# Weight splits and block sums of a dense layer made in the key-value stage and kept in DRAM, with three more weight pairs through seven block products

## The chip, the cores and the metric

The kernel runs on one core of one Trainium2 chip. Five engines of the core appear below: PE (TensorE, the matrix unit, whose weight loads are listed apart as PEld), DVE (VectorE), ACT (ScalarE), POOL (GpSimd) and SP (SyncE, which here only issues DMAs). Arrays live in DRAM, in SBUF (128 partitions) or, for results of matmuls, in PSUM, which is made of banks of 512 fp32 numbers per partition. The metric is the time on the device of one execution, in microseconds.

## The reference

Two layers read the same input and are mixed by a gate.

```python
def A(x, wqkv, w_phi, wo):               # linear attention, H = 32 heads of 20
    q, k, v = split(x @ wqkv)            # x is 1 x 2048 x 640, wqkv 640 x 1920
    pq, pk = q @ w_phi, k @ w_phi        # per head, 20 x 20
    phi_q = concat(softmax(pq), softmax(-pq))   # 40 features a head
    phi_k = concat(softmax(pk), softmax(-pk))
    kv = einsum("bhsf,bhsd->bhfd", phi_k, v)    # summed over all 2048 tokens
    z  = einsum("bhsf->bhf", phi_k)
    o = (phi_q @ kv) / (phi_q @ z + 1e-6)
    return o @ wo                        # wo 640 x 640

def B(x, w1, w2):                        # dense layer: w1 640 x 1728, w2 1728 x 640
    return silu(x @ w1) @ w2

g = sigmoid((x * gate_w).sum(-1))
return g * A(x) + (1 - g) * B(x)
```

All in fp32. The kernel reaches that accuracy with matmuls in a faster type: every operand is *split* into a high part (a rounded copy, made on ScalarE) and a low part (the operand minus its high part, made on VectorE or POOL), and a product is three matmuls: high by high, high by low, low by high.

## The kernel before, in words

Tokens come in 16 tiles of 128 for the keys and values, and in 4 blocks of 512 for the dense layer, worked on in two halves of two blocks. The 1728 columns of `w1` (rows of `w2`) are 13 chunks of 128 and one of 64; chunks 0 to 9 form the five *pairs* p = 0..4, chunks 10 to 13 are done singly.

The stages, with their places in the trace:

- **Start**, 0 to 32 us: key and value weights are split, tiles 0 and 1 are projected.
- **Key-value stage**, 32 to about 168 us, one token tile after another. For tile t, PE projects the tile into three PSUM banks, named `kvp_75`, `kvp_76` and `kvp_77` in the orders below, of 480, 500 and 302 columns (`kv_proj`, L566, 45 matmuls); these hold the keys' features (columns 0 to 639), the values and the gate's sum. VectorE takes each head's largest and smallest feature and subtracts (`k_spikes`, L581 to L588, first for columns 0 to 479, then 480 to 639); ScalarE copies the values (`v_part`, L399) and takes the exponential (L728); VectorE sums and takes reciprocals (`k_sums`, L592, L593); POOL scales the whole tile `ek` by these (L594). Two tiles later PE adds the products of `ek` and the values to `kvt` (`kv_acc`, L553). A bank is written anew only when it has been read, so the first bank of tile t+1 waits for the first four `k_spikes` instructions of tile t. Between them, every second tile has the next tokens split (`load_x`, L192 on ScalarE, L194 on POOL), and the others one of nine weight chunks that are wanted early (`load_f`: the list `PRE`, of `w2`'s chunks 10 to 13 and of `w1`'s 0 and 10 to 13).
- **Head**, 168 to about 232 us, and then ten **periods** n = 1..10. In period n the first product of pair n (`x @ w1`, first half of the tokens for n = 0..4, second for n = 5..9) and the second product (`@ w2`) of the pair before it are made side by side.
- **Tail** (500 to 560 us) and the queries with the output projection (560 to 728 us).

The first product of a pair over a half, 2 x 2 blocks, is always made with seven block products in place of eight, Strassen's scheme in a variant: `pair_mm`, banks `a`, `b`, `c`, `d`, 54 matmuls of 128x512. It needs sums of the weights' blocks as well as the weights. `pair_weights` makes them in the first half: both row chunks are loaded, ScalarE and POOL split them, POOL forms four block sums (L862), and these are split too (L865, L866); the results are stored to DRAM (`w_d`), and `pair_weights_again` loads them in the second half.

The second product is made in one of two ways. `out_items` makes ten sums of six matmuls (60, L1053), each added to an accumulator by VectorE (L1058). `sevens` uses seven block products here too (42 matmuls, L1094, and 12 for the fifth column block, L1116: 54 in all), with evictions at L1084; it needs block sums of `w2` (`block_sums`, L918 on POOL, L923 on ScalarE, L924 on VectorE) and sums of the dense layer's middle values (`t_sum`, `t_hi`, `t_lo`). Before the change `NSEV = 4`: pairs 0 to 3 of the second half go by `sevens`, all others by `out_items`. `block_sums` runs in periods 1 to 3 of the first half, and its results too are kept in DRAM (`s_d`) for the second half.

From the head on, the order of the instructions of PE, ACT, DVE and POOL is the order in which the program is written, and that is a string of names per period: `O1` to `O10`, with `HEAD`, `PASS` (last token tile and start of the head) and `TAIL`. In them `P1m` is the matmuls of the first block product of `pair_mm` and `P1p` what follows on other engines; `6am` and `6ae` are matmuls and eviction of the sixth block product of `sevens`, column blocks a (`b`: the other two); `y0m`, `y1m` are the fifth column block's; `o3m`, `o3e` those of `out_items`; `w0` ... are steps of the weights of the next pair, `c0` ... loads of `w2`, `s0`, `s1` loads of block sums, `b0` ..., `d0` ... steps of `block_sums`, `t2`, `h2`, `l2` sums of the middle values and their high and low parts. In the key-value stage the order is kept on ACT, DVE and POOL, but not on PE, where the scheduler takes what is ready by its own estimate. SP's DMAs stand in one queue in the order in which the program comes to them.

Of the kernel before, what the change touches and what calls it, by code (L numbers as in the profile page):

```python
# [16 lines left out]
P = 128  # L17
S = 2048
D = 640
# [41 lines left out]
NEARLY = 3  # L61
TAIL = """
dm0 fl4 da0 wa fl1 fl2 fm0 fl3 dm1 fs0 fm1 fs1 fl5 da1 dm2 ol1 W fm2 da2 dm3 fm3 fs2 fs3 da3 ol3 dm4
fm4 hm012 fm5 fs4 hm013 km wb fs5 hp012 hm113 wc hm112 kp hp013 hp113 ol0 da4 qp12 q012 q112 os1 wd
hp112 qe12 im0 qn12 ol4 qs12 ia0 qN12 im1 qc12 qp13 ig0 q013 ia1 qP12 im2 qi12 q113 ia2 qw12 qe13
qs13 qm12 ol2 qc13 im3 qn13 ia3 ig1 qN13 qP13 qp14 os0 os2 ig2 qi13 q014 im4 q114 qw13 ig3 xl0 ia4
qm13 im5 os3 qe14 qs14 qn14 qc14 xl1 qp15 ia5 qN14 xs0 xs1 qP14 q015 ig4 qi14 im6 tm0 xl2 q115 tm1
to0 qw14 qm14 os4 qe15 to1 ia6 qs15 qc15 qn15 im7 ia7 ig5 tm2 im8 ig6 ia8 im9 qN15 xs2 qP15 tm3 ig7
qi15 qw15 ia9 to2 ig8 to3 ig9 qm15
"""  # L70
PASS = """
wh h0a h0b us0 h1a uh0 h1b wl ka us1 uh1 ul0 ul1 h2a h2b us2 h3a xh1 xh3 uh2 h3b xh4 xl3 kb xh0 xl0
ko0 xl1 us3 xh2 ko1 xl2 ko3 ko2 ul2 xl4
"""
HEAD = """
w0 gs P1m P1p rs r0 w1 w2 w3 P2m hm10 hm12 w4 P2p dm0 r1 ks0 w5 w6 w7 w8 s10 ks1 w9 s30 s11 hp12 da0
ks2 mg dm1 ks3 s20 w10 w11 da1 dm2 da2 s40 dm3 s31 s21 s41 da3 st p31 hm13 p10 p40 v0 p11 dm4 p20 p41
hp10 v1 hm11 hp11 hp13 v2 p21 v3 da4 P5m P5p P4m em0 p30 y0 v4 y1 y2 ea0 P4p em1 y3 P6m y4 ea1 y5 P6p
em2 P3m y6 y7 ea2 P3p y8 y9 P7m P7p em3 Cm ea3 y10 em4 y11 Cp ea4
"""  # L80
O1 = """
P1m P1p o0m b0 b1 o0e b2 b3 P2m P2p b4 b5 o1m o1e b6 b7 P5m P5p st b8 c0 o2m o2e c1 c2 c3 P4m P4p d0
o3m o3e d1 d2 P6m P6p d3 d4 o4m o4e d5 d6 P3m P3p d7 d8 o5m o5e P7m w0 w1 P7p w2 w3 o6m o6e w4 w5 o7m
o7e w6 w7 o8m o8e w8 w9 Cm Cp w10 w11 o9m o9e
"""
O2 = """
P1m o0m P1p c0 c1 o0e c2 c3 P2m P2p d0 d1 o1m o1e d2 d3 P5m P5p st d4 d5 o2m o2e d6 d7 P4m P4p w0 o3m
d8 o3e w1 P6m w2 P6p w3 w4 o4m o4e w5 w6 P3m P3p w7 w8 o5m o5e w9 w10 P7m P7p w11 o6m o6e o7m o7e o8m
o8e Cm Cp o9m o9e
"""  # L90
O3 = """
xl2 xl1 P1m P1p xl0 o0m c0 xu0 o0e o1m P2m o1e xu1 P2p c1 xu2 P5m st c2 P5p c3 o2m o2e d0 d1 P4m P4p
d2 d3 o3m d4 d5 o3e P6m P6p o4m d6 d7 o4e d8 w0 P3m P3p w1 w2 o5m o5e w3 w4 P7m P7p w5 w6 o6m o6e w7
w8 o7m o7e w9 o8m w10 o8e w11 Cm Cp o9m o9e
"""
O4 = """
r0 P1m P1p o0m g c0 o0e c1 P2m P2p r1 c2 o1m st s10 o1e c3 P5m o2m P5p o2e s11 P4m w0 P4p s30 w1 o3m
o3e s31 w2 P6m P6p s20 w3 o4m o4e s21 s40 P3m p10 P3p o5m s41 o5e p11 p40 P7m P7p p41 xl4 o6m o6e xu4
o7m o7e p21 p20 xl3 o8m o8e xu3 Cm Cp o9m o9e
"""  # L100
O5 = """
P1m P1p p30 p31 o0m o0e yl4 yu4 o1m o1e yl2 yu2 o2m o2e P2m P2p c0 yl3 yu3 c1 o3m w0 w1 P5m P5p st w2
w3 o3e o4m o4e P4m P4p P6m P6p o5m o5e P3m P3p o6m o6e P7m P7p o7m o7e o8m o8e Cm Cp o9m o9e
"""
# [30 lines left out]
def mix_kernel(ctx: ExitStack, tc: tile.TileContext, xT, wqT, wkc, wkr, wv, bd, bdc, cst, wo, w1, w1r, w2, out):  # L135
# [1697 lines left out]
```

## Time and profile before

| what | value |
|---|---|
| time, median of 3 runs | 730.0 us (729.78 to 730.61) |
| the profiled execution: its own time | 730.17 us |
| its span, first to last instruction | 728.4 us |
| granted TensorE clock, as a share of full speed | 1.00 |
| PE busy | 721.2 us, 99% of the span |
| DVE, POOL, ACT busy | 429.9, 395.6, 297.4 us |
| DMA | 98.80 MB, mean 136 GB/s |

Engines' rows give busy time, its share of the span and the number of instructions. In the tables by stage each row is a stretch of the span; after its length stand, for PE, PEld, DVE, ACT and POOL, busy time and number of instructions, then the granted clock, the busy share of the DMA engines and the GB/s moved. In the chain (the work that ended last, followed back) and in the timelines a row has its start, how long it took, and what it was, with `x6` for six instructions; what stands in brackets is how long the engine was idle before it and for whom it waited.

### The profile page before, as it was taken

To read this page: it belongs to the slowest core of one execution; us is meant where nothing else is said; L and a number is where in the kernel's file an instruction comes from. 1 tells how busy PE (TensorE), PEld (TensorE's weight loads), DVE (VectorE), ACT (ScalarE), POOL (GpSimd) and SP (SyncE) were. 2 spreads that over 40 slices of the span, in tenths; PEclk is the share of its full clock that TensorE was granted. 3 is DMA by queue.
4 is the path that set the end of the run, shared out by engine and by line. 5 is a ranking of instruction groups with operands and counts; after the bars stand their busy time and mean duration, and the time that the engine had idled before them with its cause. 6 is when DMAs were issued, how large, how long until landed. Compare 5 with 4: busy or idle time off the path is not lost.

```text
span 728.4 us, 12513 instructions
## 1 busy us (share of the span) xinstructions
PE 721.2 (99%) x4935; PEld 621.0 (85%) x4935; DVE 429.9 (59%) x708; ACT 297.4 (41%) x558; POOL 395.6 (54%) x307
## 2 busy tenths in 40 slices
PE   9999999999999999999999999999999999999998
PEld 8888888888888888888888788788997899999988
DVE  4565555565253557568525656653887766766652
ACT  5333322336466354435344323535334453435330
POOL 2354545534756475572766447311598867767440
PEclk9999999999999999999999999999999999999999
DMA  8111111114734577588965623342133332121222
GB/s 306 56 56 56 46 56 55 63 35 135 238 116 176 213 276 277 207 314 324 330 205 188 219 68 107 109 117 73 52 115 119 102 95 83 56 94 45 74 87 81
DMA packets 50751, 98.80 MB, mean 136 GB/s; under 512 B 6352, under 2 KB 25828, under 8 KB 50692
## 3 DMA queue, kind: packets, MB, share of 16 engines
q1 hardware_dynamic: 50692, 98.00, 40.0%
q8 instruction: 39, 0.64, 0.4%
q14 instruction: 20, 0.16, 0.1%
HBM read 66.15 MB, written 31.84 MB: 135 GB/s over the span
## 4 chain that ended last, share of the span: by engine, by line
PE 97%; DVE 1%; ACT 1%; DMA 1%; issue 0%; DVEq 0%; ACTq 0%
PE o L1053 18%; PE kvp L566 17%; PE pa L1629 10%; PE pq L542 9%; PE a L964 9%; PE o L1094 5%; PE ph L632 3%; PE c L964 3%; PE b L964 3%; PE d L964 3%; PE pn L1587 3%; PE pT L1480 2%; PE hp L651 2%; PE kvt L553 2%; PE o_m L1116 1%; PE kvp L440 1%
## 5 line engine op out<-in xcount | busy, mean ns | idle before, releaser
L1053 PE MATMUL o<-u,w 128*128 128x512 f32 x580 | 142.5, 391 | 0.0
L1053 PEld LDWEIGHTS o<-u,w 128*128 128x128 f32 x580 | 108.0, 188 | 22.7 <-DVE acc L1058 0.6
L566 PE MATMUL kvp<-wh,xa 128*128 128x480 f32 (+2 forms) x420 | 92.5, 360 | 0.0
L566 PEld LDWEIGHTS kvp<-wh,xa 128*128 128x128 f32 x420 | 72.8, 188 | 10.4
L1629 PE MATMUL pa<-oT,wo 128*128 128x256 f32 x600 | 77.1, 281 | 0.1
L363 POOL TENSOR_TENSOR w<-wr,w 128x640 fp32r<-128x640 f32 x26 | 41.8, 1615 | 64.5 <-ACT w L352 64.5
L1629 PEld LDWEIGHTS pa<-oT,wo 128*128 128x128 f32 x600 | 73.8, 188 | 1.1 <-DVE oT L1608 0.8
L1209 POOL TENSOR_TENSOR ez<-eq,zbc 128x1280 f32<-128x1280 f32 x16 | 48.0, 3002 | 47.6 <-DVE sm L1239 24.6
L594 POOL TENSOR_TENSOR ek<-ek,st 128x1280 f32<-128x1280 f32 x16 | 38.2, 2386 | 50.3 <-DVE st L593 42.1
L542 PE MATMUL pq<-wq,xb 128*128 128x320 f32 x360 | 55.9, 312 | 0.0
L542 PEld LDWEIGHTS pq<-wq,xb 128*128 128x128 f32 x360 | 52.9, 188 | 2.2 <-DVE oT L1608 2.0
L1058 DVE TENSOR_TENSOR acc<-acc,o 128x512 f32<-128x512 f32 x70 | 46.4, 679 | 14.2 <-PE o L1053 14.1
L978 ACT ACTIVATE v<-v 128x512 f32<-128x512 f32 x33 | 20.9, 632 | 82.9 <-DVE v L997 36.2
L194 POOL TENSOR_TENSOR xa<-xra,xa 128x512 fp32r<-128x512 f32 (+1 forms) x26 | 26.4, 1038 | 41.4 <-ACT xa L192 37.0
L566 PE MATMUL kvp<-wl,xa 128*128 128x480 f32 (+2 forms) x210 | 47.6, 356 | 0.0
L1192 ACT ACTIVATE eq<-eq 128x1280 f32<-128x1280 f32 x16 | 20.4, 1276 | 63.9 <-DVE eq L533 63.9
L980 DVE TENSOR_TENSOR u<-v,u 128x512 fp32r<-128x512 f32 x29 | 21.5, 742 | 34.4 <-ACT u L979 31.5
L399 ACT COPY v<-kvp 128x340 f32<-128x340 f32 (+1 forms) x30 | 12.5, 417 | 70.1 <-PE kvp L566 68.2
L566 PEld LDWEIGHTS kvp<-wl,xa 128*128 128x128 f32 x210 | 36.6, 188 | 4.8
L1084 DVE TENSOR_TENSOR acc<-acc,o 128x512 f32<-128x512 f32 x48 | 31.3, 682 | 15.6 <-PE o L1094 12.1
L1245 POOL TENSOR_TENSOR eq<-eq,sm 128x1280 f32<-128x1280 f32 x16 | 37.9, 2368 | 1.0 <-DVE sm L1239 0.8
L592 DVE TENSOR_REDUCE st<-ek 128x64 f32<-128x1280 f32 x16 | 23.8, 1487 | 22.7 <-ACT ek L728 21.3
(236 smaller groups left out, 1483.7 us busy)
## 6 DMA issues: line engine op xcount, KB each, us to landing
wr<-w SPq DMA_DIRECT2D x33, 320.0 KB
w_d<-w SPq DMA_DIRECT2D x15, 640.0 KB
xr<-xT SPq DMA_DIRECT2D x27, 256.0 KB
w<-w_d SPq DMA_DIRECT2D x10, 640.0 KB
fb_d<-acc SPq DMA_DIRECT2D x20, 256.0 KB
s_d<-s SPq DMA_DIRECT2D x8, 512.0 KB
sa<-s_d SPq DMA_DIRECT2D x8, 512.0 KB
y<-fb_d SPq DMA_DIRECT2D x16, 256.0 KB
```

What stands on the lines that cost most here:

```text
L363: eng.tensor_tensor(t[:, 1, :], r[:, :D], t[:, 0, :].bitcast(F32), op=ALU.subtract)
L542: nc.tensor.matmul(dst, xt[c][:, hx, :], w[:, c, hw, lo : lo + n], start=first, stop=(hx == 1 and c == NC - 1))
L566: nc.tensor.matmul(kv_cols(t, lo, hi), xt[c][:, hx, :], WKV[hw][:, c, w_cols(lo, hi)], start=(n == 0), stop=(n == 3 * NC - 1), skip_group_ ...
L594: nc.gpsimd.tensor_tensor(groups(e), groups(e), spread(st[:, 1, :]), op=ALU.mult)
L964: last["mm"] = nc.tensor.matmul(out, lhs, rhs, start=(first and i == 0), stop=(stop and i == len(todo) - 1), skip_group_check=True)
L1053: nc.tensor.matmul(o, lhs, rhs, start=(n == 0), stop=(n == len(todo) - 1))
L1058: nc.vector.tensor_tensor(acc[j][m], acc[j][m], o, op=ALU.add)
L1084: nc.vector.tensor_tensor(acc[j][m], acc[j][m], o, op=ALU.add)
L1094: nc.tensor.matmul(o, ws[hw], x()[hx], start=(first and i == 0), stop=(i == len(PASSES) - 1), skip_group_check=True)
L1209: nc.gpsimd.tensor_tensor(ez, Q[t]["e"], zbc, op=ALU.mult)
L1245: nc.gpsimd.tensor_tensor(groups(q["e"]), groups(q["e"]), spread(q["sm"][:, 2 * H : 4 * H]), op=ALU.mult)
L1629: nc.tensor.matmul(pa[:, a, :], wo_tile[0][:, c, hw, ds] if c < NG else WOR[:, ds], o[:, ho, c, :] if c < NG else o[:GW, ho, c, :], start= ...
```

## The change

Nothing is computed otherwise than before except that three more second products go by `sevens`; the rest is a move of work from the first half to the key-value stage.

- `NSEV = (3, 4)`: pairs 0 to 2 of the first half and 0 to 3 of the second go by `sevens`. PE's rows fall from 4267 to 4249 matmuls, those of `out_items` from 580 to 400, those of `sevens` rise from 168 to 294 and from 48 to 84.
- A new generator `weights_ahead` runs in the key-value stage. For pairs 1 to 4 it loads two chunks of `w1`, splits the first whole (`F`, 128x640) and the second's last 384 columns (`B`), makes four block sums on POOL (`R10` is sum 0 of pair 1) and splits these (`G`, 128x256 each); for pairs 0 to 4 it loads two chunks of `w2` and splits them (`U`), and for pairs 0 to 3 makes and splits the four block sums (`S`, `Y`). The high parts are copies on ScalarE, the low parts subtractions on VectorE. All go to DRAM. There are 14 splits of 128x640, 4 of 128x384, 32 of 128x256, and 32 block sums of 128x256; VectorE's instructions rise from 710 to 755 over the kernel, ACT's from 559 to 563, POOL's go from 310 to 298, SP's from 299 to 340.
- The order of the key-value stage is now a string `KV`: `T4` is the projection of tile 4 and the `kv_acc` of tile 2, `a4` and `b4` the two parts of `k_spikes`, `v4` the values, `e4` the exponential, `r4` sums and reciprocals, `m4` POOL's scaling, which is now placed apart from `r4`, `x4` and `l5` are `load_x` and `load_f`.
- The nine early chunks are stored to DRAM as well (`w_keep`) and loaded again where they were split a second time (`w_again`). In the first half `pair_weights_again`, `w2_again` and `sums_again` load what was made; `pair_weights` remains for n = 0 and n = 10, and the stores and `block_sums` of the first half are gone.
- All strings of orders are written anew.

Three places in the instructions' order follow. The first is VectorE in the key-value stage, from tile 4's maxima to tile 5's first (`mmk` holds the maxima and minima, `ek` the features, `st` the sums). Before:

```order
L581 TENSOR_REDUCE mmk_690<-kvp_75 128x24
L582 TENSOR_REDUCE mmk_690<-kvp_75 128x24
L587 TENSOR_TENSOR ek_691<-kvp_75,mmk_690 128x24x20
L588 TENSOR_TENSOR ek_691<-mmk_690,kvp_75 128x24x20
L581 TENSOR_REDUCE mmk_690<-kvp_76 128x8
L582 TENSOR_REDUCE mmk_690<-kvp_76 128x8
L587 TENSOR_TENSOR ek_691<-kvp_76,mmk_690 128x8x20
L588 TENSOR_TENSOR ek_691<-mmk_690,kvp_76 128x8x20
L592 TENSOR_REDUCE st_718<-ek_691 128x64
L593 RECIPROCAL st_718<-st_718 128x64
L581 TENSOR_REDUCE mmk_800<-kvp_75 128x24
```

After, from the last subtraction of tile 4 (`ra` are raw weight rows, `aw`, `awb`, `awc`, `awd` the tiles of split weights):

```order
L612 TENSOR_TENSOR ek_772<-mmk_771,kvp_76 128x8x20
L769 TENSOR_TENSOR aw_783<-ra_2_667,aw_783 128x640
L769 TENSOR_TENSOR awb_785<-ra_3_669,awb_785 128x384
L769 TENSOR_TENSOR awb_785<-ra_3_669,awb_785 128x256
L769 TENSOR_TENSOR awc_800<-ra_2_667,awc_800 128x256
L769 TENSOR_TENSOR awc_800<-ra_3_669,awc_800 128x256
L769 TENSOR_TENSOR awd_806<-ra_2_667,awd_806 128x256
L616 TENSOR_REDUCE st_827<-ek_772 128x64
L617 RECIPROCAL st_827<-st_827 128x64
L605 TENSOR_REDUCE mmk_909<-kvp_75 128x24
```

Six subtractions of weights now stand between tile 4's features and its sums, and ahead of tile 5's maxima.

The second place is PE at the start of tile 6 in the key-value stage (`wh`, `wl` are the parts of the key and value weights, `xa` the tokens). Before:

```order
L553 MATMUL kvt<-ek_482,v_103 21x40 x32
L566 MATMUL kvp_75<-wh,xa_0_704 128x480 x2
L566 MATMUL kvp_75<-wh,xa_2_709 128x480 x2
L566 MATMUL kvp_75<-wh,xa_4_714 128x480
L566 MATMUL kvp_75<-wl,xa_0_704 128x480 x2
```

After:

```order
L577 MATMUL kvt<-ek_534,v_112 21x40 x32
L590 MATMUL kvp_77<-wh,xa_0_813 128x302 x2
L590 MATMUL kvp_77<-wh,xa_2_818 128x302 x2
L590 MATMUL kvp_77<-wh,xa_4_823 128x302
L590 MATMUL kvp_77<-wl,xa_0_813 128x302 x2
L590 MATMUL kvp_77<-wl,xa_2_818 128x302 x2
L590 MATMUL kvp_77<-wl,xa_4_823 128x302
L590 MATMUL kvp_77<-wh,xa_0_813 128x302 x2
L590 MATMUL kvp_77<-wh,xa_2_818 128x302 x2
L590 MATMUL kvp_77<-wh,xa_4_823 128x302
L590 MATMUL kvp_75<-wh,xa_0_813 128x480 x2
```

The third bank is now filled first in tile 6, as it is in tile 13 and, for 10 of its 15 matmuls, in tile 3.

The third place is PE in period 7, a period of the second half that goes by `sevens` before and after (`o1_10` and `o1_11` are the banks of block product 1 for the column blocks a and b, to which products 6 and 5 are added; `ts0` and `ts1` are middle sums, `sa1_0` block sums of `w2`). Before:

```order
L1116 MATMUL o1_m1_3946<-u6_3_1_3850,w2_3_3735 128x512 x3
L1094 MATMUL o1_10_3881<-ts0_3597,sa1_0_3862 128x512 x3
L964 MATMUL a7_3854<-xo0_1871,wc7_3675 128x512 x6
L1094 MATMUL o1_11_3874<-ts0_3597,sa1_0_3862 128x512 x3
L1094 MATMUL o1_10_3881<-ts1_3598,sa1_0_3862 128x512 x3
L1094 MATMUL o1_11_3874<-ts1_3598,sa1_0_3862 128x512 x3
```

After:

```order
L1070 MATMUL d7_4055<-xf_2_4_3552,wb7_3793 128x512 x3
L1200 MATMUL o1_10_3995<-ts0_3711,sa1_0_3976 128x512 x3
L1200 MATMUL o1_11_3979<-ts0_3711,sa1_0_3976 128x512 x3
L1070 MATMUL a7_3968<-xo0_2162,wc7_3794 128x512 x6
L1200 MATMUL o1_10_3995<-ts1_3712,sa1_0_3976 128x512 x3
L1200 MATMUL o1_11_3979<-ts1_3712,sa1_0_3976 128x512 x3
```

The six matmuls of `pair_mm`'s sixth block product have moved between the two products that write `o1_10` and `o1_11`. On VectorE the eviction between these two products (`acc0_1`, second row) stood behind both evictions of the fifth column block (`acc0_4`, `acc1_4`); before:

```order
L1084 TENSOR_TENSOR acc0_4_2067<-acc0_4_2067,o1_m0_3926 128x512
L1084 TENSOR_TENSOR acc1_4_2071<-acc1_4_2071,o1_m1_3946 128x512
L1084 TENSOR_TENSOR acc0_1_2064<-acc0_1_2064,o1_10_3881 128x512
L1084 TENSOR_TENSOR acc0_3_2066<-acc0_3_2066,o1_11_3874 128x512
L1084 TENSOR_TENSOR acc1_1_2073<-acc1_1_2073,o1_10_3881 128x512
```

After it stands between them:

```order
L1103 TENSOR_TENSOR v1_7_3992<-v1_7_3992,b7_4006 128x512
L1190 TENSOR_TENSOR acc0_4_2359<-acc0_4_2359,o1_m0_4040 128x512
L1190 TENSOR_TENSOR acc0_1_2356<-acc0_1_2356,o1_10_3995 128x512
L1190 TENSOR_TENSOR acc1_4_2363<-acc1_4_2363,o1_m1_4047 128x512
L1190 TENSOR_TENSOR acc0_3_2358<-acc0_3_2358,o1_11_3979 128x512
```

It has moved ahead of one eviction. The diff, cut to its core:

```diff
-NSEV = 4
+NSEV = (3, 4)
+KV = """
...
+S02 S03 a3 b3 Y03h v3 R1 Y00h e3 Y00l Y02h Y03l Y02l Y01h Y01l m2 r3 m3 l3 T4 a4 b4 v4 F1h B1h e4 F1l
+B1l R10 R11 R12 Q1 R13 G13h G10h G13l G12h G10l G11h G12l G11l x4 r4 m4 T5 a5 b5 v5 U10h U11h e5 U11l
...
 O7 = """
-P1m t3 s0 w0 2am t2 1bm P1p 2ae 1am 1be 1ae 2bm h3 P2m st h2 s1 w1 P2p t4 l2 c0 2be P5m c1 P5p y0m
...
+P1m t3 s0 t2 1bm w0 2am P1p 2ae 1am 1be 1ae 2bm h3 P2m h2 w1 P2p c0 s1 t4 l2 2be P5m c1 P5p y0m y1m
...
+    def w_again(w, f, pool=None):
+        t = W[w, f] = w_tile(w, f, pool)
+        with tc.issue_after(last["x"].ins):
+            nc.sync.dma_start(w_flat(w, f, t), w_k[w, f] if (w, f) in w_k else w2_d[f].rearrange("p s d -> p (s d)"))
...
-        nc.gpsimd.tensor_tensor(groups(e), groups(e), spread(st[:, 1, :]), op=ALU.mult)
+        return lambda: nc.gpsimd.tensor_tensor(groups(e), groups(e), spread(st[:, 1, :]), op=ALU.mult)
...
+    def weights_ahead(ops):
+
+        def row(w, f):
+            r = ta.tile([P, D], F32, tag="wr", name=f"ra{w}_{f}", bufs=4)
+            nc.sync.dma_start(r, w1[f] if w == 1 else w2[f * P : (f + 1) * P, :])
+            return r
+
+        def out(name, n):
+            return ta.tile([P, 2 * D], F32R, tag="wk", name=name, bufs=3)[:, :n]
...
+            def hi():
+                d[:] = dst()
+                nc.scalar.copy(d[0], src())
+
+            def lo():
+                eng.tensor_tensor(d[1], src(), d[0].bitcast(F32), op=ALU.subtract)
+                if done:
+                    keep(*done())
...
+                        nc.gpsimd.tensor_tensor(q[i], q[a], q[b], op=op)
...
     with inorder(ACT, DVE, POOL):
-        for t in range(NT - 1):
+        ops, scaled = {}, {}
...
+        weights_ahead(ops)
+        for name in KV.split():
...
+            ops.pop(name)()
...
     def pair_weights(n):
...
-        p = n if n < NPAIR - 1 else n - (NPAIR - 1)
+        p = n and NPAIR - 1
...
-        sev = NPAIR - 1 <= n < NPAIR - 1 + NSEV
+        sev = n < 2 * NPAIR - 2 and p < NSEV[h]
...
-            if NPAIR - 1 < n < NPAIR + NSEV:
+            if n < 2 * NPAIR - 2 and n != NPAIR - 1 and q < NSEV[n > NPAIR - 1]:
                 sevens(q, n == NPAIR)
...
-            if NPAIR - 2 < n < 2 * NPAIR - 2:
-                named("c0 c1", w2_again(2 * p, 2 * p + 1))
-            else:
-                named("c0 c1 c2 c3", w2_loads(2 * p, 2 * p + 1))
-            if NPAIR - 3 < n < 2 * NPAIR - 3:
+            named("c0 c1", w2_again(2 * p, 2 * p + 1))
+            if n < 2 * NPAIR - 3:
                 named("w0 w1 w2 w3", pair_weights_again(n + 1))
...
-            if n == 1:
-                named(" ".join(f"b{k}" for k in range(9)), block_sums(0))
-            if n < NSEV:
-                named(" ".join(f"d{k}" for k in range(9)), block_sums(n))
```

341 lines of the change are left out of this document (195 added, 146 removed).

## Prediction

> **What bounds the kernel now.** I read the engines' totals first, then PE's waits, then the table by stage, then the chain and single tiles. The totals of the page:
>
> ```profile
> span 728.4 us, 12513 instructions
> ...
> PE 721.2 (99%) x4935; PEld 621.0 (85%) x4935; DVE 429.9 (59%) x708; ACT 297.4 (41%) x558; POOL 395.6 (54%) x307
> ```
>
> PE is busy for all but 7.2 us. Its listed waits, first and last of five, the longest 1.1 us:
>
> ```profile
> PE warm L410 <- DVE ones L234: 1.1, 1, 1.1
> ...
> PE a L964 <- DVE v L1027: 0.2, 1, 0.2
> ```
>
> No large stall is there to remove, so only fewer matmuls or shorter gaps between them can save time, and a new wait anywhere adds in full. The table by stage has the key-value stage, the last two periods of the first half and the first two of the second:
>
> ```profile
> 61.00:168.00 107.00, 107.00 (x1222) 92.75 (x1209) 63.73 (x114) 35.10 (x71) 50.95 (x33) 1.00 0.20 58
> ...
> 314.00:340.00 26.00, 26.00 (x115) 21.13 (x114) 18.79 (x28) 11.54 (x22) 10.58 (x8) 1.00 0.91 330
> 340.00:366.00 26.00, 26.00 (x117) 21.50 (x116) 16.58 (x25) 8.29 (x15) 19.32 (x14) 1.00 0.92 335
> ...
> 391.00:416.00 25.00, 24.90 (x109) 19.87 (x108) 14.92 (x24) 8.34 (x14) 12.95 (x11) 1.00 0.52 170
> ```
>
> In the key-value stage PE is never idle, the others are busy 60% (DVE), 33% (ACT) and 48% (POOL), and DMA moves 58 GB/s. The granted clock is 1.00 in all rows, so no term below comes from it.
>
> **Fewer matmuls.** The chain has the price of one and the length of the periods (start, duration, what):
>
> ```profile
> 245.22 1.36 PE o L1053 x6
> ...
> 283.52 1.36 PE a L964 x6
> ...
> 309.36 1.36 PE a L964 x6
> ...
> 361.37 1.36 PE a L964 x6
> ...
> 385.51 2.04 PE a L964 x9
> ...
> 410.59 2.04 PE a L964 x9
> ...
> 435.80 2.04 PE a L964 x9
> ...
> 462.11 1.36 PE a L964 x6
> ```
>
> Six matmuls in 1.36 us are 0.2267 us each. From 283.52 to 309.36 a period by `out_items` takes 25.84, which is its 54 + 60 = 114 matmuls at that price: PE has no gap there. By `sevens` it has 108. Three pairs more are 18 matmuls fewer, **-4.08 us**, all of it on the path, since PE sets the end.
>
> But the four periods that go by `sevens` now are not gapless. Rows with x9 hold three matmuls of the last product ahead of the new pair's six, so those pairs begin 0.68 later, at 386.19, 411.27 and 436.48. The periods last 24.82, 25.08, 25.21 and 25.63; 108 matmuls are 24.48. Lost are 0.34, 0.60, 0.73 and 1.15, together 2.82. One of the places, from the chain in period 7:
>
> ```profile
> 400.67 0.69 PE o L1094 x3
> 401.37 0.02 issue
> 401.39 0.70 DVE acc L1084
> 402.09 0.04 issue
> 402.13 0.96 PE o L1094 x3
> ```
>
> PE waits 0.76 for VectorE to empty a bank to which the next product is added. I take for each of the three new periods the smallest loss seen, 0.34, as their orders are of the same kind as the new ones of the second half: **+1.02 us**; the bounds are 0 and 1.15 each (0 to 3.45). They have less to do besides than the periods of before: block sums and splits are gone from them.
>
> **The new orders of the second half.** In period 7 six matmuls of `pair_mm` (1.36 us) now stand between the two products, and the bank's eviction has moved ahead of another of 0.70. It can begin when its product ends and is done after 0.70 plus what is left of the one before: at most 1.4 us, against 1.36 of cover. The wait of 0.76 should go nearly whole. I take all four periods at 0.34, a gain of 0.26 + 0.39 + 0.81 = **-1.46 us**; bounds are no gap at all (-2.82) and new gaps of the same size as the old elsewhere (+0.5, about one stall of the kind).
>
> **The work in the key-value stage.** Before, one tile there (80.47 to 90.11) looks like this: projection from the chain, then rows of single engines (what stands in brackets is idle time and its cause):
>
> ```profile
> 80.47 8.93 PE kvp L566 x45
> 90.11 8.93 PE kvp L566 x45
> ```
>
> ```profile
> 81.59 3.24 POOL L194 TENSOR_TENSOR xa<-xra,xa 128x512 fp32r<-128x512 f32 x3 [4.45 <-ACT xa L192]
> 84.78 2.37 POOL L594 TENSOR_TENSOR ek<-ek,st 128x1280 f32<-128x1280 f32 x1
> ```
>
> ```profile
> 83.96 0.66 DVE L581 TENSOR_REDUCE mmk<-kvp 128x24 f32<-128x480 f32 x1 [1.16 <-PE kvp L566]
> ...
> 85.67 0.64 DVE L588 TENSOR_TENSOR ek<-mmk,kvp 128x480 f32<-128x480 f32 x1
> 87.90 0.33 DVE L581 TENSOR_REDUCE mmk<-kvp 128x8 f32<-128x160 f32 x1 [1.59 <-ACT v L399]
> ...
> 90.32 1.49 DVE L592 TENSOR_REDUCE st<-ek 128x64 f32<-128x1280 f32 x1 [1.41 <-ACT ek L728]
> 91.84 0.55 DVE L593 RECIPROCAL st<-st 128x64 f32<-128x64 f32 x1
> ```
>
> A tile lasts 9.65 us. By the stage's row VectorE works 63.73/107 of it, 5.75 us; ScalarE 3.17; POOL 4.60. Prices for what is added, from the same instructions elsewhere (duration in ns: least, median, most):
>
> ```profile
> L924 DVE TENSOR_TENSOR s<-wr,s x16: 410/420/1781, 235.0 to 300.8; 128x256 fp32r<-128x256 f32 x16
> ```
>
> ```profile
> L194 DVE TENSOR_TENSOR wo<-wo,wo x5: 815/875/2568, 514.3 to 546.0; 128x640 fp32r<-128x640 f32 x5
> L194 DVE TENSOR_TENSOR xf<-xrf,xf x4: 628/676/2850, 159.9 to 163.8; 128x512 fp32r<-128x512 f32 x4
> ```
>
> ```profile
> L352 ACT CAST w<-wr x28: 712/732/743, 35.9 to 508.5; 128x640 fp32r<-128x640 f32 x28
> ```
>
> ```profile
> L923 ACT CAST s<-wr x16: 400/402/407, 234.1 to 299.9; 128x256 fp32r<-128x256 f32 x16
> ```
>
> ```profile
> L862 POOL TENSOR_TENSOR wr<-wr x12: 733/740/1072, 190.4 to 453.3; 128x256 f32<-128x256 f32 x12
> ```
>
> 128x384 lies between, by length about 0.55 on VectorE and 0.51 on ScalarE. VectorE: 14 x 0.815 + 4 x 0.55 + 32 x 0.42 = 27.0; ScalarE: 14 x 0.732 + 4 x 0.51 + 32 x 0.402 = 25.1; POOL: 32 x 0.74 = 23.7. Over the 13 tiles 2 to 14 that is 2.1, 1.9 and 1.8 a tile, and the engines come to 7.85, 5.1 and 6.4 of 9.65 us. None is full, so by sums alone the work hides behind PE.
>
> By its place it is tight. The bank that tile t+1 fills first is free when tile t's first four `k_spikes` are done, and the scaled features are wanted two tiles later. I walked the orders of the engines through tiles 4 to 6 with these prices, counted from tile 4's start. Tile 4's last `k_spikes` end at about 8.6; ScalarE's copy of values, exponential and weight copies follow; POOL's four block sums run to about 14.8; the last of the six subtractions, behind them, ends at 15.8; sums and reciprocals at 18.0; tile 5's first maxima, free since about 13, only then run and end at 20.35. Tile 6 starts at 19.3: with the first bank first it would wait 1.1 us. With the third bank first, as the order of PE has it, 15 of 45 matmuls go ahead (302 of 1282 columns of 8.93 us, 2.1 us), the first bank is wanted at 21.4, and 1.0 is left. The same walk leaves about 0.35 at tile 8, 0.9 at tiles 9 and 13, 0.6 at tile 15. So no stall, but little room. Behind a late `a` part stand on VectorE `b`, the next subtractions and `r`; for `r` waits POOL's `m`, and for that `kv_acc` on PE.
>
> DMA: loads of 18 chunks of 0.328 MB (5.9), stores of 8.39 (`w1`), 6.55 (`w2`), 4.19 (block sums) and 5.57 (early chunks), 30.6 MB over 135 us, 226 GB/s on top of 58. The 284 are less than the 335 that the period at 340 moved at a share of 0.92 with PE full. On SP, token loads now stand behind stores that wait for a late split; they come a tile and more ahead of use. I take **+0.5 us** for the stage, one slip of the smallest rooms. The lower bound is 0 (PE was full before); the upper comes with the first rival.
>
> **The rest, at zero.** Removing splits and block sums from head and first half frees ACT, DVE and POOL where PE didn't wait for them. In their place come loads: a period moves about 4.5 MB, some 178 GB/s, less than before. At the head's end 2.2 MB of weights and block sums must come after slots are free; at 330 GB/s that is 6.7 us, and they are wanted from 12 us on. Without that cover half a transfer, some 3 us, would show. Tail and queries keep their matmuls.
>
> **Sum**: -4.08 + 1.02 - 1.46 + 0.5 = -4.0. On the profiled 730.17 that is 726.2; it stood 0.17 above the median, so **726.0** against 730.0. A difference under 0.2% (1.5 us) is about what can't be told from no change.
>
> **Rivals.** *First, slower: VectorE and POOL exclude each other in the key-value stage.* The row of `xf` above, and these of the same moment:
>
> ```profile
> 159.91 4.60 DVE L194 TENSOR_TENSOR xf<-xrf,xf 128x512 fp32r<-128x512 f32 x4
> ```
>
> ```profile
> 160.16 2.59 POOL L594 TENSOR_TENSOR ek<-ek,st 128x1280 f32<-128x1280 f32 x1 [5.83 <-DVE st L593]
> ```
>
> Four subtractions with both inputs in SBUF should last 4 x 0.63 = 2.5; one took 2.85, as long as POOL's scaling beside it, and all four 4.60. The new subtractions are of this kind; `k_spikes`, which read PSUM, ran at their usual 0.64 beside POOL at 85.67. POOL's 6.4 and VectorE's 2.1 of such work come to 8.5 of 9.65 a tile: possible only if they interleave well. VectorE has 9.65 - 7.85 = 1.8 to spare. Placed at random, 3.85 subtractions a tile would meet POOL at work two times in three and wait half of about 1.7 us: 2.2, over the spare by 0.4. If one whole scaling (2.4) is waited out in each tile, the stage grows by 0.6 x 13 = 7.8, and the sum by 7.3: 733.3. From 1.8 of blocking a tile it decides. Against it: the scalings are placed apart from the subtractions (`m` behind `r`), and the block sums of a pair just ahead of the splits that need them, so that most meetings are ordered ones, which the walk holds already.
>
> [...]
>
> *Second, no change: the new `sevens` periods stall as period 9 does* (1.15 each, 3.45), and the second half's stalls only move. -4.08 + 3.45 + 0 + 0.5 = -0.1: 729.9. For it: each added order has as many bank hand-overs as the old. Against it: period 6 lost only 0.34.
>
> *Third, more gain: all gaps go*, and the stage costs nothing. -4.08 - 2.82 = -6.9: 723.1. For it: periods by `out_items` have no gap at all.
>
> **Chances and range.** Forecast 0.55 (its own range 724.0 to 728.2: stage 0 to 2.5, new periods 0.1 to 0.6 each), first rival 0.22, second 0.10, third 0.13. The first gives anything from 728 to 737; a range of 723.0 to 732.5 leaves out somewhat over half of it and a little of the third, 0.16. Faster: 0.55 + 0.13 = 0.68. Same: the second and a tenth of the first, 0.12. Slower: 0.20.
>
> **What would show it.** Right: about 4249 matmuls at 0.227; key-value tiles still 9.65 apart; periods 1 to 3 near 24.8; periods 6 to 9 near 24.8. Wrong: waits of PE's `kvp` for VectorE's `ek` or of `kvt` for POOL, tiles of more than 10 us, weight subtractions of 1.5 to 3 us beside POOL's scaling (first rival); waits for `acc` in periods 2 to 4 (second). What would upset the sum besides is a load late in period 1.

## The result, and the profile after

| | before | after |
|---|---|---|
| median of 11 runs | 730.02 us (729.39 to 730.94) | 726.63 us (724.69 to 730.02) |
| profiled execution: time, span | 730.17, 728.4 | 724.69, 722.9 |
| ratio of the times | | 0.9951, 95% interval 0.9940 to 0.9962 |

The change makes the kernel 3.4 us faster; 726.0 us had been forecast. The profiled execution of after is the fastest of its eleven, and the two further profiles of the same kernel (e1 and e11 below, 727.3 and 727.2 us) are the slowest of five and the second slowest of six, so the median lies between them. The totals on the page of after:

```profile
span 722.9 us, 12592 instructions
...
PE 715.9 (99%) x4917; PEld 617.5 (85%) x4917; DVE 462.1 (64%) x754; ACT 300.1 (42%) x563; POOL 386.3 (53%) x295
```

PE has 18 matmuls fewer (4935 before, 4917 after), is busy for 5.3 us less and idle for 7.0 in place of 7.2. The table by stage, with the columns of the one in the prediction:

```profile
61.00:168.00 107.00, 107.00 (x1277) 93.12 (x1267) 88.27 (x152) 54.07 (x112) 73.87 (x60) 1.00 0.79 284
314.00:340.00 26.00, 25.60 (x113) 20.90 (x112) 20.66 (x31) 12.76 (x23) 8.87 (x7) 1.00 0.61 225
340.00:366.00 26.00, 26.00 (x116) 21.52 (x116) 13.70 (x19) 8.55 (x15) 22.04 (x17) 1.00 0.93 344
391.00:416.00 25.00, 25.00 (x110) 20.23 (x110) 13.04 (x21) 8.34 (x14) 13.44 (x11) 1.00 0.51 179
```

In the key-value stage (first row) VectorE has gone from 63.73 to 88.27 us of 107, POOL from 50.95 to 73.87, DMA from 58 to 284 GB/s, and PE is still never idle. The chain of after, at the starts of periods 2, 3, 4, 5, 6 and 7 (a row with x9 again holds three matmuls of the product before, and the pair begins 0.68 later; in the row of 2.33 us 0.97 later, as it also holds a pause of 0.29):

```profile
254.55 2.04 PE a L1070 x9
...
279.37 2.04 PE a L1070 x9
...
304.55 2.33 PE a L1070 x9
...
332.06 1.36 PE a L1070 x6
...
357.90 1.36 PE a L1070 x6
...
381.70 2.04 PE a L1070 x9
```

The first matmuls of the stages, as PE's timelines have them, give the length of each part, for the two profiles and for e1 and e11, two more of after (us; the last row ends with the last matmul):

| part | before | after | e1 | e11 |
|---|---|---|---|---|
| start, to tile 2 | 31.93 | 32.32 | 32.64 | 32.92 |
| tile 2 to pair 0 (key-value stage) | 149.63 | 148.35 | 149.29 | 149.54 |
| head, to period 1 | 49.90 | 49.92 | 50.44 | 49.93 |
| periods 1 to 3 | 77.74 | 74.76 | 74.74 | 74.77 |
| period 4 | 25.84 | 26.54 | 26.55 | 26.55 |
| period 5 | 26.17 | 25.85 | 25.84 | 25.84 |
| periods 6 to 9 | 100.74 | 99.14 | 99.12 | 99.10 |
| period 10, to the tail | 31.71 | 32.06 | 32.04 | 32.04 |
| tail and queries | 231.38 | 230.67 | 231.56 | 231.45 |

Periods 1 to 3 and 6 to 9 repeat within 0.04 us and hold the gain, 3.0 and 1.6 us. The three new periods take 24.48, 24.82 and 25.46: against 24.48 by count they lose 0.00, 0.34 and 0.98. Start, key-value stage, head and tail differ between executions of one and the same kernel by up to 1.2 us.

One new wait has appeared, in period 4. The timelines of PE, VectorE and POOL there:

```profile
330.40 1.66 PE L1159 MATMUL o<-u,w 128*128 128x512 f32 x6 [0.40 <-DVE acc L1164]
```

```profile
324.59 1.73 DVE L1086 TENSOR_TENSOR u<-v,u 128x512 fp32r<-128x512 f32 x1 [1.35 <-ACT u L1085]
...
329.05 0.69 DVE L1086 TENSOR_TENSOR u<-v,u 128x512 fp32r<-128x512 f32 x1 [1.41 <-ACT u L1085]
```

```profile
323.23 2.54 POOL L974 TENSOR_TENSOR xr<-xr 128x512 f32<-128x512 f32 x2
```

A subtraction of VectorE with both inputs in SBUF takes 1.73 us and ends at 326.3, beside POOL's sums of tokens, in place of the 0.69 of the same line at 329.05. The evictions behind it come late, and PE waits; the chain runs through these rows from 322.56 to 330.40.

### The profile page after: what moved, and what is told of

Same layout as the page of the kernel before. It is cut to its first block, busy times and chain, and to the rows that moved or that the text cites. A ratio compares the mean times of both kernels' runs of the same rounds, so it can differ in the third digit from the quotient of the medians.

```text
span 722.9 us, 12592 instructions
## 1 busy us (share of the span) xinstructions
PE 715.9 (99%) x4917; PEld 617.5 (85%) x4917; DVE 462.1 (64%) x754; ACT 300.1 (42%) x563; POOL 386.3 (53%) x295
## 4 chain that ended last, share of the span: by engine, by line
PE 93%; DMA 2%; DVE 2%; ACT 1%; POOL 1%; issue 1%; SPq 0%; POOLq 0%; DVEq 0%; ACTq 0%
PE kvp L590 17%; PE o L1159 12%; PE pa L1723 11%; PE pq L566 9%; PE a L1070 9%; PE o L1200 9%; PE ph L656 3%; PE b L1070 3%; PE c L1070 3%; PE d L1070 3%; PE pn L1681 3%; PE o_m L1222 3%; PE pT L1574 2%; PE hp L675 2%; PE kvt L577 2%; PE kvp L464 1%
## 5 line engine op out<-in xcount | busy, mean ns | idle before, releaser
L1159 PE MATMUL o<-u,w 128*128 128x512 f32 x400 | 97.4, 392 | 0.5 <-DVE acc L1164 0.4
L590 PE MATMUL kvp<-wh,xa 128*128 128x302 f32 (+2 forms) x420 | 91.8, 358 | 0.0
L1159 PEld LDWEIGHTS o<-u,w 128*128 128x128 f32 x400 | 74.3, 188 | 16.3 <-DVE acc L1164 0.8
L1190 DVE TENSOR_TENSOR acc<-acc,o 128x512 f32<-128x512 f32 x90 | 59.2, 682 | 32.0 <-PE o L1200 29.2
L1086 POOL TENSOR_TENSOR u<-v,u 128x512 fp32r<-128x512 f32 x14 | 18.1, 1290 | 64.0 <-ACT u L1085 64.0
L590 PE MATMUL kvp<-wl,xa 128*128 128x302 f32 (+2 forms) x210 | 47.6, 355 | 0.0
L1054 POOL TENSOR_TENSOR v<-v,v 128x512 f32<-128x512 f32 x28 | 36.5, 1302 | 12.6 <-DVE u L1086 6.9
L1233 POOL TENSOR_TENSOR acc<-acc,G 128x512 f32<-128x512 f32 x20 | 28.2, 1427 | 13.6 <-DVE acc L1164 13.6
L1318 DVE TENSOR_REDUCE sm<-ez 128x64 f32<-128x1280 f32 x16 | 23.8, 1486 | 17.0 <-POOL ez L1315 17.0
```

The costliest lines, as they stand in the source:

```text
L590: nc.tensor.matmul(kv_cols(t, lo, hi), xt[c][:, hx, :], WKV[hw][:, c, w_cols(lo, hi)], start=(n == 0), stop=(n == 3 * NC - 1), skip_group_ ...
L1054: nc.gpsimd.tensor_tensor(v[i], v[a], v[b], op=ALU.subtract)
L1086: eng.tensor_tensor(u[:, 1, :], v, u[:, 0, :].bitcast(F32), op=ALU.subtract)
L1159: nc.tensor.matmul(o, lhs, rhs, start=(n == 0), stop=(n == len(todo) - 1))
L1190: nc.vector.tensor_tensor(acc[j][m], acc[j][m], o, op=ALU.add)
```

## The experiments

**e1, the changed kernel again.** No edit.

> The changed kernel once more, unedited, for a second profile. Its runs lie between 724.7 and 730.0 us, those of the kernel before between 729.4 and 730.9; the profiled one was the fastest, 724.7. Theory of the prediction: the key-value stage has little room, so the slower executions lose 1 to 2 us there, in one or two tiles longer than 9.6 us, with PE waiting for VectorE or POOL. Rival: they lose it where the chain of the fast execution already runs through a transfer (start, and the token loads at 555 to 563 us) or through POOL's sums beside VectorE in period 4; then all tiles stay at 9.58 us and the start, period 4 or the tail is longer by 1 to 2 us.

Measured: 726.39 us, ratio 0.9947 (0.9934 to 0.9959). Both expectations were partly wrong. The key-value tiles stayed at 9.6 us, as the rival had it, and nothing of the loss lies in period 4. But against the first profile 0.9 us were lost at the end of the key-value stage, where the theory had put them, though for no engine that the profile names:

```profile
166.76 0.71 PE L577 MATMUL kvt<-ek,v 128*21 128x40 f32 x56
168.33 0.27 PE L577 MATMUL kvt<-ek,v 128*21 128x40 f32 x8 [0.86 <-issue]
```

PE stops for 0.86 us in the midst of 64 like matmuls, and the profile names no engine for which it waits. The rest of the 2.6 us between the two spans is 0.3 at the start, 0.5 in the head and 0.9 in the tail. The tail's part is a wait for ScalarE (`fT`) that the kernel before has too, with 0.7, and the first profile of after has not.

**e2, the three pairs of the first half not by seven products.**

```diff
-NSEV = (3, 4)
+NSEV = (0, 4)
 O1 = """
...
+P1m P1p o0m o0e P2m P2p o1m o1e P5m P5p c0 o2m o2e c1 P4m P4p o3m o3e P6m P6p o4m o4e P3m P3p w0 o5m
+o5e P7m w1 P7p w2 w3 o6m o6e o7m o7e o8m o8e Cm Cp o9m o9e
```

(`O2` and `O3` likewise.)

> NSEV = (0, 4): the key-value stage's work, the stores and the loads stay as in the changed kernel, but the three pairs of the first half go by ten sums of six again, in the order of the kernel before with the steps left out that no longer exist. Theory of the prediction: 18 matmuls more, 4.08 us, against the 1.33 that periods 1 to 3 lose in gaps in the profile of the changed kernel (74.77 us from period 1 to 4, 73.44 by count): 2.7 us slower than the changed kernel, periods 1 to 3 again 25.84 each. Rival: the three pairs bring less than that, since freed periods have other stalls (period 4 lost 0.7); then it is within 1 us of the changed kernel.

Measured: 729.26 us, ratio 0.9986 (0.9978 to 0.9995); 2.9 us slower than the changed kernel of the same batch (e1), 2.6 than in the result. Periods 1 to 3 take 77.52 us in place of 74.76. So the 18 matmuls, less the gaps that their order brings, are worth what the profile of before said, and the rival falls.

**e3, only the new orders of periods 6 to 9 in the kernel before.** The strings `O6` to `O9` are those of the changed kernel, with the store step `st` kept behind `P2p`.

```diff
 O7 = """
-P1m t3 s0 w0 2am t2 1bm P1p 2ae 1am 1be 1ae 2bm h3 P2m st h2 s1 w1 P2p t4 l2 c0 2be P5m c1 P5p y0m
...
+P1m t3 s0 t2 1bm w0 2am P1p 2ae 1am 1be 1ae 2bm h3 P2m h2 w1 P2p st c0 s1 t4 l2 2be P5m c1 P5p y0m
```

> The kernel before with only the four order strings of periods 6 to 9 taken from the changed kernel. Theory of the prediction: the gaps in these periods shrink by the order alone, 1.5 us faster than the kernel before (728.5), the stretch from the start of period 6 to that of period 10 falls from 100.74 to about 99.2 us. Rival: the gaps shrank in the changed kernel because its loads lie otherwise and less is asked of the engines; then it is as before, within 0.5 us, and the stretch stays above 100.3.

Measured: 728.62 us, ratio 0.9979 (0.9969 to 0.9988); the stretch is 99.11 us. The order alone gives this gain. In the stage table of this kernel the same 25 us as in the prediction (391 to 416) have no idle time left:

```profile
391.00:416.00 25.00, 25.00 (x111) 20.26 (x110) 15.36 (x25) 8.34 (x14) 13.55 (x11) 1.00 0.53 184
```

**e4, no weights' work in the key-value stage.**

```diff
-        weights_ahead(ops)
         for name in KV.split():
...
-                nc.sync.dma_start(SW[q][k].bitcast(F32), s_d[q][k])
+                nc.sync.dma_start(SW[q][k].bitcast(F32), w_k[2, 10][:, :1024])
```

(`KV` loses the names of this work, and the other loads are redirected in the same way.)

> The changed kernel without the weights' work in the key-value stage: no loads of weight rows, splits, block sums and stores of these there; the later loads read other kept weights of the same size, so the dense layer's output is not the reference's. All else stands. Theory of the prediction: the work costs about 0.5 us in that stage, so this is 0.5 us faster than the changed kernel, tiles at 9.58 as in its profile. First rival of the prediction in a weak form: VectorE and POOL hold each other up in some executions, then it is 1 to 3 us faster and its runs scatter as little as those of the kernel before. Third: the work is free and the spread of the times is from elsewhere: same median within 0.4 us and same spread.

Measured: 724.99 us (724.44 to 725.98), ratio 0.9930 (0.9918 to 0.9943). The work costs 1.4 us against the changed kernel of the same batch (e1, 726.39) and 1.6 against the 726.63 of the result, three times the 0.5 forecast. The spread did not go with it: five runs of e4 lie within 1.5 us, the five of e1 within 1.7. The cost is of the size that the weak form of the first rival gave; whether that is its cause, e7 tells.

**e7, the work without its stores.** Weight rows are loaded, split and summed as in the changed kernel, and the results dropped; the later loads go to other kept weights, as in e4.

```diff
         def keep(d, t):
-            nc.sync.dma_start(d if len(d.shape) == 2 else d.rearrange("p s d -> p (s d)"), t.bitcast(F32))
+            pass
```

> The changed kernel with the weights' rows loaded, split and summed in the key-value stage as before, but these results not stored (19 MB less to DRAM); the later loads read other kept weights of the same size, so the dense layer's output is not the reference's. Without any of this work the time was 725.0, with all of it 726.5. Theory now: the 1.5 us come from the transfers (start, late token and weight loads at the end of the stage, PE's own instruction fetch), not from the engines; then this comes near 725.0 to 725.5. Rival: they come from the engines' work; then it stays at 726.2 to 726.7.

Measured: 725.10 us, ratio 0.9927 (0.9914 to 0.9940), the time of e4. The two kernels in the key-value stage, first e4 and then e7:

```profile
61.00:168.00 107.00, 107.00 (x1265) 92.81 (x1265) 62.45 (x110) 34.93 (x68) 51.66 (x33) 1.00 0.29 96
```

```profile
61.00:168.00 107.00, 107.00 (x1264) 92.59 (x1265) 86.99 (x153) 53.76 (x112) 73.78 (x61) 1.00 0.43 137
```

24.5 us more of VectorE, 18.8 of ScalarE and 22.1 of POOL cost nothing in the median. The cost goes with the 19 MB of stores: by the ratios to the kernel before, 0.9930 and 0.9927 against 0.9947 to 0.9958 in the three batches of the changed kernel, 1.2 to 2.3 us. (Both kernels also read the later loads from other places; periods 1 to 9 take the same time in them as in after within 0.1 us, so nothing of the cost lies there.)

Only a part of it has been found in a place. The tiles don't get longer by the stores: from tile 2 to tile 15 e7 and e11 take 124.30 us each. What e7 and e4 lack is PE's stop in `kvt`: 0.65 to 0.86 us in e1, e8, e9 and e11, 0.4 in e2, all with stores; the first profile of after, e5, e6 and e10 have stores and no such stop. The difference at the start is not from the stores, of which the first is issued at 35.8 us in after and 36.1 in e1.

The packets of the DMA trace suggest what PE waits for in this stop. It stands ahead of the same matmul in all five, the 953rd of `kvt`, and 1.2 to 1.4 us before PE goes on, a packet of 16 KB of queue q8, kind "instruction", has come to its end: 166.89 and 168.33 in e1, 167.61 and 168.86 in e11. The queue has 39 such packets per execution, one for about 250 of PE's matmuls and weight loads (4917 of each in after), so I take them for PE's own instructions; that is an inference from the count. In the kernels without these stores (before, e3, e4, e7) this packet starts when PE has begun about 1600 matmuls; in the five it starts after 1683 to 1692. In the first profile of after it is as late (1684), but PE, which passes there at 167.06, has it at 165.96. So the stop fits instructions that come late. Why they do is not shown: e6 and e10 store as much and have the packet in time (1598 and 1616).

**e5, VectorE's subtractions beside POOL's scaling.** In the string `KV` each `G..l`, `Y..l` and `U..l` is moved behind the next `r`; for tile 4:

```diff
-B1l R10 R11 R12 Q1 R13 G13h G10h G13l G12h G10l G11h G12l G11l x4 r4 m4 T5
+B1l R10 R11 R12 Q1 R13 G13h G10h G12h G11h x4 r4 G13l G10l G12l G11l m4 T5
```

The low parts `U` are then taken from rows that already hold block sums, so the output isn't the reference's.

> The changed kernel with one edit of the key-value stage's order: the low parts G, Y and U (VectorE's subtractions of weights) stand behind the tile's sums and reciprocals r instead of ahead of them, so on VectorE they come just when POOL begins that tile's scaling m. First rival of the prediction (VectorE and POOL exclude each other): the first of these subtractions in a tile lasts as long as the scaling, about 2.4 us instead of 0.42 or 0.82; VectorE then has 7.85 + 2 of 9.58 us a tile to do, PE waits for kvp, and the stage is 3 to 8 us longer (729 to 734). If the two don't exclude each other, or only where one happens to start first: subtractions stay at 0.42 and 0.82, and the time is that of the changed kernel, 726.5.

Measured: 747.25 us, ratio 1.0230 (1.0211 to 1.0250): as the first rival had it, with a larger loss than was worked out. The timelines of VectorE, POOL and PE, the first two and the last row ahead of tile 8:

```profile
87.62 6.08 DVE L769 TENSOR_TENSOR as<-ra,as 128x256 fp32r<-128x256 f32 x4
```

```profile
87.31 3.61 POOL L207 TENSOR_TENSOR xa<-xra,xa 128x512 fp32r<-128x512 f32 x3
90.88 2.54 POOL L618 TENSOR_TENSOR ek<-ek,st 128x1280 f32<-128x1280 f32 x1
```

```profile
62.39 1.35 PE L590 MATMUL kvp<-wh,xa 128*128 128x480 f32 x5 [1.79 <-DVE ek L612]
...
96.10 2.34 PE L590 MATMUL kvp<-wh,xa 128*128 128x480 f32 x5 [4.88 <-DVE ek L612]
```

Four subtractions of 0.42 us take 6.08, about as long as POOL's token split and scaling together (3.61 + 2.54); `k_spikes` stand behind them, and PE waits 4.88 us. From 32 to 190 us 49 of the 50 subtractions took 50.5 us, against 33.05 for all in the changed kernel and 27.0 by the prices in the prediction. The table by stretches shows the second half of the price, in the column of the granted clock:

```profile
91.00:96.10 5.10, 0.23 (x25) 0.12 (x11) 5.10 (x7) 0.33 (x2) 4.00 (x3) 0.80 0.57 207
96.10:99.00 2.90, 2.90 (x7) 2.45 (x8) 1.50 (x5) 2.09 (x4) 0.00 (x0) 0.50 0.98 338
99.00:102.00 3.00, 3.00 (x12) 2.57 (x11) 2.96 (x4) 0.79 (x2) 1.50 (x1) 0.69 0.27 100
102.00:110.00 8.00, 8.00 (x103) 6.93 (x102) 5.00 (x11) 3.52 (x9) 3.39 (x4) 1.00 0.83 292
```

After the long wait PE is granted 0.50 of its clock for 2.9 us and 0.69 on the mean of the next 3; the tile's 45 matmuls took 11.15 us in place of 8.9. After the wait of 1.79 five matmuls took their usual 1.35.

**e10, only the block sums' low parts beside the scaling.** As e5, with `U` left in its place.

```diff
-U10l r5 S10 S11 l5 Y12h S12 S13 T6 R2 a6 b6 v6 Y10h m5 Y13h F2h B2h F2l e6 Y10l Y12l B2l R20 R21 Y13l
-Y11h Y11l x6 r6 m6
+U10l r5 S10 S11 l5 Y12h S12 S13 T6 R2 a6 b6 v6 Y10h m5 Y13h F2h B2h F2l e6 B2l R20 R21
+Y11h x6 r6 Y10l Y12l Y13l Y11l m6
```

> As the run with the low parts beside the scaling, but with only the low parts of the block sums (G, Y: 32 of 128x256) behind r; U stays where the changed kernel has it. There VectorE's subtractions took 50.5 us in place of 33.05, the stage 171.7 in place of 148.4, with two waits of about 5 us after which PE ran at a granted clock of 0.5 for some 5 us. Theory: exclusion of VectorE by POOL, paid where a group of four subtractions meets the scaling and the token splits; these groups (Y in tiles 5, 8, 10) are still there, so most of the loss stays: 738 to 745 us. Rival: the loss came from U, whose rows are then held longer and whose block sums come late; then it is below 732.

Measured: 741.99 us, ratio 1.0167 (1.0153 to 1.0182). The 32 small subtractions carry most of the loss, and the rival falls.

**e6, PE in the program's order.**

```diff
-    with inorder(ACT, DVE, POOL):
+    with inorder(PE, ACT, DVE, POOL):
         ops, scaled = {}, {}
```

> The changed kernel with PE too held to the order of the program in the key-value stage, so that tiles 3, 6 and 13 begin with the first bank of the projection and not with the third. Theory of the prediction (hand walk): tile 6 then waits about 1.1 us for the first bank and tile 13 about as much, since VectorE's maxima of the tile before come late: 1 to 2.5 us slower than the changed kernel, PE waits on kvp for DVE ek near 90 us and 157 us. Rival: in the profile of the changed kernel VectorE had more room than the walk gave it (it took the sums of tile 5 at 84.8 and tile 6's first maxima at 86.8, with PE far from the bank's next use); then there is no wait and the time is the same within 0.5 us.

Measured: 729.49 us, ratio 0.9989 (0.9981 to 0.9998); 2.9 us slower than the changed kernel's 726.63. PE's timeline has three waits, at the starts of tiles 6 and 13 and in a `kvt` behind POOL:

```profile
72.34 1.32 PE L590 MATMUL kvp<-wh,xa 128*128 128x480 f32 x5 [0.77 <-DVE ek L612]
...
140.49 1.36 PE L590 MATMUL kvp<-wh,xa 128*128 128x480 f32 x5 [0.99 <-DVE ek L612]
...
160.87 0.78 PE L577 MATMUL kvt<-ek,v 128*21 128x40 f32 x64 [1.74 <-POOL ek L618]
```

The walk had said 1.1 us for each of the first two; the place was right (70 and 140 us; the "90" and "157" of the expectation were misplaced) and the size nearly. The third was not foreseen. The profiled execution took 731.70 us, at a granted clock of 0.997 over its span; behind the third wait PE's clock is halved for 3.41 us (last section).

**e8, weight rows later and the old order of period 4.**

```diff
+            with tc.issue_after(last["kw", 2].ins):
+                nc.sync.dma_start(r, w1[f] if w == 1 else w2[f * P : (f + 1) * P, :])
...
 O4 = """
-g P1m P1p c0 r0 o0m o0e c1 P2m P2p r1 o1m w0 o1e P5m P5p w1 s10 o2m o2e s11 o3m P4m P4p s30 o3e s20
...
+r0 P1m P1p o0m g c0 o0e c1 P2m P2p r1 o1m s10 o1e P5m o2m P5p o2e s11 P4m w0 P4p s30 w1 o3m o3e s31
```

> A candidate: the changed kernel with two edits. The first four rows of weights are loaded only after the third chunk's key weights have been multiplied (about 14 us), so they don't share the DMA engines with the start's own weights; and period 4 has the order of the kernel before (without the steps that no longer exist). Theory: the start reaches tile 2 at 32.1 instead of 32.5 to 32.8 us, and period 4 lasts 25.84 instead of 26.54: about 1.2 us faster than the changed kernel, 725.3. Rival: the transfers are only moved to a place where they are as much in the way, and period 4's wait for VectorE beside POOL's sums comes back in another row: the time is the same within 0.4 us.

Measured: 727.53 us, ratio 0.9956 (0.9944 to 0.9968), no gain over the changed kernel. Period 4 is indeed down to 25.86, but period 5 up from 25.85 to 26.47: the wait moved, as the rival had it. The start reached tile 2 at 32.88, so the weight rows were not what delays it. The traces say so too: in e1 PE's wait there, 0.88 us for ScalarE's part of the key weights, ends at 9.5, and the first weight row is issued at 11.5.

**e9, token loads ahead of a store.**

```diff
-        w_keep(w, f)
+        (held.append((w, f)) if n in (6, NPRE - 1) else w_keep(w, f))
...
-        ops["xf"] = lambda: [next(xf0) for _ in range(4)]
+        ops["xf"] = lambda: ([next(xf0) for _ in range(4)], [w_keep(*held.pop(0)) for _ in range(len(held))])
```

> A candidate: the changed kernel with one store moved on SP: the last two of the nine early chunks are stored behind the first half's token loads, so the third token load no longer stands behind a store that waits for POOL's late split. In a slow execution of the changed kernel the chain at the end of the key-value stage runs through these: split, store, token load, splits of tokens, first weights of pair 0, and the head took 50.44 instead of 49.92 us. Theory: the head is again at 49.9 in the profile and the median falls by 0.3 to 0.7 us against the changed kernel of the same batch. Rival: what costs is the amount stored (without the 19 MB of stores the time fell by 1.4 us), not one place in SP's queue: no difference beyond 0.3 us.

**e11, the changed kernel in the same batch.**

> The changed kernel unedited, in the same batch as the candidate, for the comparison and a third profile: 726.5 us; the stage from tile 2 to the head between 148.3 and 149.3 us, period 4 at 26.5, periods 6 to 9 at 99.1.

Measured: both 727.04 us, ratio 0.9958 (0.9946 to 0.9970). Against its expectation e11 is 0.5 us slower and its stage, 149.54, a little outside; periods 4 and 6 to 9 are as expected. The head of e9 took 49.90 us, but that of e11 49.93 too, and both have the stop in `kvt`. This place in SP's queue is not the cause. Neither e8 nor e9 beats the changed kernel.

## Why the prediction came out right

*Fewer matmuls, -4.08 us less new gaps of 1.02.* Measured -2.98 in the stage table against -3.06; e2 gives the same from the other side, 2.8 by its periods and 2.6 to 2.9 by the medians. The count is right by its mechanism. That the gaps came to 1.3 us where 1.02 was taken is partly luck: 0.34 was taken for each period, and they were 0.00, 0.34 and 0.98, the last well outside the 0.1 to 0.6 given.

*New orders of the second half, -1.46.* Measured -1.60, and -1.63 in e3, where nothing else was changed. The step in question, six matmuls laid between two products that share a bank, did what it should: period 7 had lost 0.60 and loses nothing now. The quoted wait of 0.76 was read too large. From 401.19 to 402.03 PE made three matmuls of the other column block; by the starts of the matmuls the bank cost 0.37. The sum was not built on the 0.76. Here too the single periods differ from the 0.34 taken for each: 6 and 7 lose nothing, 8 and 9 together 1.2.

*The key-value stage, +0.5: mis-sized, and for another reason than was given.* It measured 1.4 to 1.6 (e4), 1.2 to 2.3 by the ratios. The prediction looked for it among the engines, in the smallest rooms of its walk. Engine work there is free (e7 against e4). What costs is the stores; I had compared 284 GB/s with the 335 moved in period 5 and taken the difference for room. Of the loss only PE's stop at the stage's end is located, 0.4 to 0.9 us in five of the profiles; it fits the late packet of queue q8, and moving one store (e9) didn't remove it. Where the rest lies stays open.

*The first rival* was a sound warning and lost by placement. The prediction gave it a chance of 0.22 with a price of 7.3 us. With the subtractions placed beside the scaling (e5, e10) it is real and 15 to 21 us large. The price was low for two reasons: VectorE's subtractions last longer beside POOL's token splits too, not only beside the scaling (in e5 four took 6.08 us beside 3.61 + 2.54), and behind the wait of 4.88 us the tile took a further 2.2 at the lowered clock (11.15 - 8.9). In the changed kernel the subtractions are longer as well, 33.05 - 27.0 = 6.0 us over 13 tiles, 0.46 each against a room of 1.8 (the longest took 2.27 us). Why a subtraction lasts that long beside POOL is not shown by these runs.

*The walk through tiles 4 to 6* said that tile 6 needs its third bank first. e6 shows it: 0.77 and 0.99 us where 1.1 was expected.

*At zero I had put periods 4, 5 and 10 and the tail.* Period 4 lost 0.70, period 5 gained 0.32, period 10 lost 0.35: +0.7 together. Period 4 shows the same in another place (1.73 us beside POOL in place of 0.69), which the prediction weighed only for the key-value stage. Period 10's loss is not one of the change alone: with the same order there it takes 32.0 in after, e1, e11, e6 and e8, but 31.7, as before, in e2, e4, e5, e7, e9 and e10. The 0.34 is a wait for a VectorE eviction at its first `o` product; why only some have it was not found.

Together, by the terms, for e1 and e11: -2.98 - 1.60 + 0.73 + 1.0 (start, stage, head and tail) = -2.9, where the forecast sum was -4.0 and the medians moved by -3.4; in the first profile the last term is -1.6. The two terms that carry the gain came to -4.58 against a forecast of -4.52.

That the whole came within 0.6 us is partly luck. The stores and period 4 were undercounted, and against them stood a gain that nobody had counted: with none of the work in it (e4) the stage in its new order takes 149.01 us against 149.63 before. Of that 0.40 is tile 3, which takes 10.00 us in before and e3 and 9.60 in after, e1, e11 and e4.

## What to carry to other kernels

When PE is busy throughout, count matmuls first, then the gaps between them; both sums came out within 0.2 us from the chain alone, though the single periods did not. Work moved under a full PE may be free by its sum and ruinous by its order: look where VectorE's subtractions with both inputs in SBUF meet POOL's long instructions (in e5 one of 0.41 us took 2.60 beside a scaling of 2.36), and at what follows PE's waits (in e6, behind one of 1.74 us, five matmuls took 1.83 us in place of 1.35). Price stores apart from engine work, by a kernel that drops them.

## What was not expected of the hardware

A wait of PE can cost more than its length. After 1.79 us (e5) five matmuls took 1.35 us, after 4.88 they took 2.34, with a granted clock of 0.50 in the 2.9 us that follow. The length of the wait alone doesn't tell. In e10 it happened behind one of 3.13 us, and in e6 behind one of 1.74: the second row has the 64 small matmuls behind that wait, the next two the first ten of the tile, which elsewhere take 1.35 and 1.25:

```profile
93.93 1.88 PE L590 MATMUL kvp<-wh,xa 128*128 128x480 f32 x5 [3.13 <-DVE ek L612]
```

```profile
160.87 0.78 PE L577 MATMUL kvt<-ek,v 128*21 128x40 f32 x64 [1.74 <-POOL ek L618]
161.59 1.83 PE L590 MATMUL kvp<-wh,xa 128*128 128x480 f32 x5
163.22 2.20 PE L590 MATMUL kvp<-wl,xa 128*128 128x480 f32 x5
```

But behind 1.79 us in e5 and 2.09 in e10 the first five took their usual 1.35 and 1.36. In the clock's records the stretches at half speed last 3.41 us (e6 and one of e10) or 6.83 (the other of e10 and both of e5), and the first of e5 begins 2.8 us after its wait did (its row above has 0.80 from 91.00 to 96.10). The granted clock over the whole span is 0.997 in e6, 0.993 in e10 and 0.991 in e5. What sets these lengths is not shown.

In the first profile and in e1 most of PE's tiles in the key-value stage are shorter than before, not longer: 8.87 us for 45 matmuls where before has 8.93. The additional work is not the reason. In e11, the same kernel, most tiles take 8.93 again, and in e7, with the same engine work, the tiles are as long as in e11 to 0.01 us. PE's load queue has 12 separate semaphore instructions of 51 ns there in all three executions of the changed kernel, and 21 before, so these don't explain it either. The cause is open.
